# Retention attention into a squared-ReLU feed-forward: smaller loads and memsets, a later copy and sum, and two start-up casts on ScalarE

## The chip, the cores and the metric

The kernel runs on one core of a Trainium2 chip. The metric is the device time of one execution in microseconds (us). A core has five engines that run their own instruction streams in order and meet through semaphores: TensorE (PE, with its weight loads shown apart as PEld), VectorE (DVE), ScalarE (ACT), GpSimd (POOL) and SyncE (SP, which here only issues transfers). Transfers run on the core's 16 DMA engines.

## The reference, cut to what matters

Two stages. The first is a recurrent attention over 4 batches, 8 heads, 768 tokens and 64 channels; the second is a feed-forward layer over all 3072 tokens.

```python
gamma = 1.0 - 2.0 ** (-5.0 - np.arange(H))            # one decay for each head
for t in range(S):
    state = gamma * state + outer(k[t], v[t])         # 64 x 64 for each batch and head
    y[t] = scale * q[t] @ state
x = y.transpose(0, 2, 1, 3).reshape(B * S, H * D)     # 3072 x 512
h = np.maximum(x @ w_in, 0.0)                         # w_in: 512 x 2048
out = h * h @ w_out                                   # w_out: 2048 x 512
```

## The kernel before

The recurrence is computed in chunks of 128 tokens, 24 in all. Inside a chunk the attention is a masked product of scores and v; between chunks a state is carried in PSUM (`c_ps`) and copied to bf16 (`s_bd`). The decays are folded into q, k and, later, v, by scaling them with powers of gamma. The results `xt` of a block of chunks feed the feed-forward: `first_product` (L847) multiplies by w_in, ACT applies the ReLU (L856), DVE squares (L827), and the second product multiplies by w_out. The first block holds four chunks, the others two each.

The second product of a pair of chunks is made from seven half-size products and sums of their operands. For the first block this is `last_of_first`: it treats chunks 2 and 3 this way, and chunks 0 and 1 plainly (`plain`, L1043). Its sums are made on DVE by `add` (L1004) in `first_sums`, `third_sums` and `fourth_sums`; `fourth_sums` makes s4 in two halves, x = 0 and 1, which only the last product reads. Its results leave through ACT copies to `osb` tiles and stores on SP.

Start-up. All of q's, k's and v's first four chunks come in pairs. PE multiplies by the zero tile `still` between real products (`keep_awake`, L368), which computes nothing. `cast_pair_v` (L597) casts v to bf16, by default on POOL, one call for each of two row sets r; its argument `on_scalar` would use ACT. `state_pair` (L653) needs both. `cast_w` casts a 512 x 512 group of w_in in two column halves of four chunks each, one letter per chunk: G is POOL, V is DVE, S (any other) is ACT. The first half of the first group is cast as "GGGV".

The rest is a written order. Each piece of the feed-forward is a step of a generator (`ffn_pieces`), counted by n. `put(place, what, ...)` notes work, such as a load, a scaling, a transpose, that is issued behind piece number `place`; `before(n)` issues it, in the order of the `put` calls. So each engine's stream follows from the places. `attend(5, ...)` puts the transposes of k (`transpose_k`, L430, with two ACT copies to `k_bd` at L437) at place 27, the two halves of `scores` (L456 on PE, masked by DVE at L463) at places 30 and 32, and the outputs (L532) at 34. The scores' PSUM pool `ps_st` has one buffer, so the second half of the scores waits for the mask of the first.

Loads: `load_q(m)` (L93) loads q for two chunks, 512 KB, in one transfer on SP's queue; `load_kv` (L126) loads k or v of a chunk. `load_w_out` goes through POOL's queue. The pool memsets at L1372 clear the unused half of three `k_big` tiles, one instruction for each half of the partitions.

Of the kernel before, what the change touches and what calls it, by code (L numbers as in the profile page):

```python
# [13 lines left out]
AF = mybir.ActivationFunctionType  # L14
ALU = mybir.AluOpType
# [16 lines left out]
def kernel(  # L32
# [9 lines left out]
    nc = tc.nc  # L42
# [4 lines left out]
    C = 128  # L47
# [37 lines left out]

    raw_q, raw_k, raw_v = {}, {}, {}

    def load_q(m):

        b, i = chunks[m]  # L90
        t = ldqpool.tile([P, H, 2, D], FP32, name="qn")
        src = q[b, :, i * C : (i + 2) * C, :].rearrange("h (s r) d -> s h r d", r=2)
        nc.sync.dma_start(t[:], src)  # L93
        raw_q[m] = t

    heads_of = [slice(0, H // 2), slice(H // 2, H)]
# [250 lines left out]
    def cast_w(kind, g, halves=(0, 1), on="VVSG"):  # L347

        src = staged[kind, g]
        dst = (w_in_bf if kind == "in" else w_out_bf)[g]  # L350
        for half in halves:
            c = slice(half * 256, (half + 1) * 256)
            for j, engine in enumerate(on):
                if engine == "G":
                    nc.gpsimd.tensor_copy(dst[:, j, c], src[:, j, c])
                elif engine == "V":
                    nc.vector.tensor_copy(dst[:, j, c], src[:, j, c])
                else:
                    nc.scalar.activation(dst[:, j, c], src[:, j, c], AF.Copy)
# [3 lines left out]
    def keep_awake(n, width=4 * C, pool=ps_f, name="psf"):  # L363
        if not idle_ps:
            idle_ps.append(pool.tile([P, 4, P], FP32, name=name))
        wide = max(1, width // C)
        for _ in range(n):
            nc.tensor.matmul(  # L368
                idle_ps[0][:, 0:wide, 0 : width // wide],
                lhsT=still,  # L370
                rhs=still[:, None, 0 : width // wide].to_broadcast([P, wide, width // wide]),
                start=True,
                stop=True,
            )
# [217 lines left out]
    def cast_pair_v(m, r, on_scalar=False):  # L592
        at[m]["v"] = pair_view(v_bd2s[m // 2])
        if on_scalar:
            nc.scalar.activation(at[m]["v"][:, r], raw_v[m][:, r], AF.Copy)
        else:
            nc.gpsimd.tensor_copy(at[m]["v"][:, r], raw_v[m][:, r])  # L597
# [385 lines left out]
    def last_of_first():  # L983

        def halves_of(k, c):
            return [
                t.rearrange("e (j k) (c t) -> e k c j t", k=2, c=4)[:, k, 2 + c] for t in h2s[0]
            ]

        (a11, a12), (a21, a22) = ([halves_of(k, c) for k in range(2)] for c in range(2))  # L990
        n = NFB // 4
        s1, s2, s4 = (
            [
                t.rearrange("e (x j t) -> e x j t", x=2, t=C)[:, x]
                for x in range(2)
            ]
            for t in (spare[:, i * HN * 4 : (i + 1) * HN * 4] for i in range(3))
        )
        s3 = a21
        b = lambda k, c: lambda j: w_out_bf[j // 2][:, 2 * (j % 2) + k, c * HN : (c + 1) * HN]  # L1000
        t1, t2, t3, t4 = (lambda j, t=t: t[:, j] for t in sums)

        def add(out, in0, in1, op=ALU.add):
            nc.vector.tensor_tensor(out=out, in0=in0, in1=in1, op=op)  # L1004

        def product(to, left, right, js, start=True, stop=True):
            for j in js:
                nc.tensor.matmul(  # L1008
                    to,
                    lhsT=left[j // n][:, j % n],  # L1010
                    rhs=right(j),
                    start=(start and j == 0),
                    stop=(stop and j == NFB // 2 - 1),
                    skip_group_check=True,
                )

        def first_sums(x):
            add(s1[x], a21[x], a22[x])
            add(s2[x], s1[x], a11[x], ALU.subtract)

        def third_sums():
            for x in range(2):
                add(s3[x], a11[x], a21[x], ALU.subtract)

        def fourth_sums():
            for x in range(2):
                add(s4[x], a12[x], s2[x], ALU.subtract)

        def second_products():
            ops = [ps_f.tile([P, DM], FP32, name="psf") for _ in range(2)]  # L1030
            pa, pe, pd, pb = (
                t[:, n * HN : (n + 1) * HN]
                for t in [ps_f.tile([P, DM], FP32, name="psf") for _ in range(2)]
                for n in range(2)
            )
            oa, ob = (opool.tile([P, DM], FP32, name="osb") for _ in range(2))
            a, u, v = (upool.tile([P, HN], FP32, name=f"u{i}") for i in range(3))
            r0 = 2 * C

            def plain(j):  # L1040
                for f in (2 * j, 2 * j + 1):
                    for c, op in enumerate(ops):
                        nc.tensor.matmul(  # L1043
                            op[:],
                            lhsT=h_of(0, f)[:, 0, c * C : (c + 1) * C],
                            rhs=w_out_bf[f // FPQ][:, f % FPQ, :],
                            start=(f == 0),
                            stop=(f == NFB - 1),
                        )
                product(pa, a11, b(0, 0), (j,))  # L1050

            lo, hi = range(0, 4), range(4, 8)
            for j in range(4):
                plain(j)
                yield
            product(pd, s1, t1, lo)
            product(pb, s2, t2, lo, False)
            yield
            for j in range(4, 6):
                plain(j)  # L1060
                yield
            product(pe, a22, t4, lo, False)
            yield
            plain(6)
            yield
            plain(7)
            nc.scalar.activation(a[:], pa, AF.Copy)
            for c, op in enumerate(ops):
                osb = opool.tile([P, DM], FP32, name="osb")
                nc.scalar.activation(osb[:], op[:], AF.Copy)  # L1070
                nc.sync.dma_start(out[c * C : (c + 1) * C], osb[:])
            yield
            product(pd, s1, t1, hi)
            product(pb, s2, t2, hi)
            add(u[:], pb, a[:])
            yield
            product(pa, a12, b(1, 0), lo, False)
            yield
            product(pa, a12, b(1, 0), hi, False)
            nc.scalar.activation(oa[:, 0:HN], pa, AF.Copy)  # L1080
            yield
            product(pb, s3, t3, lo, False)
            yield
            product(pb, s3, t3, hi, False)
            add(v[:], pb, a[:])
            add(ob[:, HN:DM], pd, v[:])
            yield
            product(pe, a22, t4, hi)
            add(ob[:, 0:HN], pe, v[:])

            def last_product():
                product(pd, s4, b(1, 1), range(8), False)
                add(oa[:, HN:DM], pd, u[:])
                yield
                nc.sync.dma_start(out[r0 + C : r0 + 2 * C], ob[:])
                yield
                nc.sync.dma_start(out[r0 : r0 + C], oa[:])
                yield

            kept.append(last_product())  # L1100
            yield

        return first_sums, (third_sums, fourth_sums), second_products
# [27 lines left out]
    def ffn_pieces(tb):  # L1131
        nch = BLOCKS[tb]
        TB = nch * C
        if tb == 0:
# [1 line left out]
            put(11, first_sums, 0)  # L1136
            put(17, first_sums, 1)
            put(26, last_sums[0])
            put(27, last_sums[1])
            for f in range(FPQ, NFB):  # L1140
                hp = ps_f.tile([P, TB], FP32, name="psf")
                first_product(tb, hp[:], f, slice(0, TB))
# [97 lines left out]
    mask_b(0)  # L1240
    mask_b(1)
    keep_awake(1)
    transpose_pair_k(2, 1, *f)
    cast_pair_v(0, 0)
    cast_pair_v(0, 1)
    cast_pair_v(2, 0)
    cast_pair_v(2, 1)
    mask_a = scores_pair(2, 0, (st, f), spare[:, 0:1024])
    keep_awake(2)
    end_awake()  # L1250
    mask_a(0)
    mask_a(1)
# [2 lines left out]
    outputs_pair(0, 1)  # L1255
    mask_b = scores_pair(2, 1, (tp, f), spare[:, 1024:2048])
    mask_b(0)
    cast_w("in", 0, (0,), "GGGV")
    mask_b(1)
    finish_pair(0, 0)  # L1260
    finish_pair(0, 1)
    state_pair(0, 1, "SV")
    outputs_pair(2, 0, ((ps_y, "y"), st))
    first_pair(0)
# [20 lines left out]
    def put(place, what, *args):  # L1285
        parts.setdefault(place, []).append((what, args))
# [31 lines left out]
        put(place, load_w_out, g)  # L1318
    for m, which, place in ((4, "v", 10), (5, "k", 12), (5, "v", 14)):
        put(place, load_kv, m, which)  # L1320
    put(15, load_q, 6)
    for m, which, place in ((6, "k", 16), (6, "v", 17), (7, "k", 18), (7, "v", 19)):
        put(place, load_kv, m, which)
    put(10, cast_w, "in", 3)
# [15 lines left out]

    for j, t in enumerate(k_bigs):
        for hh in range(2):
            put((16, 34, 43)[j] + hh, nc.gpsimd.memset, t[halves[hh], :, :, 1 - hh, :], 0.0)

    put(20, load_q, 8)
    put(41, load_q, 10)
    done = [57, 62] + [70 + 8 * j for j in range(14)]

    ahead = {
# [62 lines left out]
```

## Time and profile before

| what | value |
|---|---|
| median of 3 runs | 203.47 us (203.37 to 203.81) |
| profiled execution, its own time | 203.39 us |
| its span (first to last instruction) | 201.6 us |
| busy: PE, PEld | 195.0, 164.6 us |
| busy: DVE, ACT, POOL | 151.0, 127.1, 82.7 us |
| moved by DMA | 36.02 MB, mean 179 GB/s |
| L368 warming matmuls before L653 | two, at 11.44 us on the chain |
| L430 transposes of chunk 5 | 43.06 us on the chain |

Times inside the profile count from the start of the span. Busy time of PE includes the modelled end of each pipelined matmul, so PE shown busy is not PE at its peak. A group of instructions is named by line, engine, operation, tile written and tiles read. The chain that ended last follows the end of the program back, at each step to what released it.

### The profile page before, as it was taken

The page shows a single profiled execution, that of the slowest core. Times are in us where ns is not written, and L with a number is a line of the kernel's source. Part 1 is how long each engine was busy: PE and PEld are TensorE (multiplying, and loading weights), DVE is VectorE, ACT ScalarE, POOL GpSimd, SP SyncE. Part 2 cuts the span into 40 slices and gives each one's busy share as a digit, 9 for nine tenths or more (in the row PEclk, how much of TensorE's full clock was granted, in tenths as well). Part 3 has the DMA queues.
Part 4 walks back from the last instruction along what each step waited for, and adds up shares of the span by engine and source line. Part 5 has one row for each costly group of instructions (what it writes and reads, how often), then busy time and mean ns, then how long its engine had stood idle before and what let it go on. Part 6 is the DMA issues. An engine that isn't in the chain of part 4 may idle for free.

```text
span 201.6 us, 5846 instructions
## 1 busy us (share of the span) xinstructions
PE 195.0 (97%) x2362; PEld 164.6 (82%) x2362; DVE 151.0 (75%) x327; ACT 127.1 (63%) x258; POOL 82.7 (41%) x150
## 2 busy tenths in 40 slices
PE   7799999999999999999999999999999999999991
PEld 2468445779988999899999999999999999999881
DVE  3986899799598886777687697697696696484472
ACT  8864875264863666774766866864865865845710
POOL 8683760899930762154422185116362202200000
PEclk9999999999999999999999999999999999999999
DMA  5999999999987999599979399999999762101102
GB/s 166 356 375 397 343 192 196 252 201 227 305 174 182 176 163 238 172 134 180 189 152 206 114 170 221 158 242 141 192 153 140 197 94 67 66 0 52 55 0 106
DMA packets 92250, 36.02 MB, mean 179 GB/s; under 512 B 68544, under 2 KB 88256, under 8 KB 92224
## 3 DMA queue, kind: packets, MB, share of 16 engines
q1 hardware_dynamic: 73088, 31.47, 66.5%
q0 software_dynamic: 19136, 4.20, 23.3%
q8 instruction: 18, 0.29, 0.6%
q14 instruction: 8, 0.07, 0.1%
HBM read 27.26 MB, written 6.29 MB: 166 GB/s over the span
## 4 chain that ended last, share of the span: by engine, by line
PE 91%; DVE 4%; DMA 2%; issue 1%; ACT 0%; DVEq 0%
PE psf L847 42%; PE psf L884 21%; PE tp L884 7%; PE psf L1043 3%; PE psf L1008 2%; DMA qn<-in_q_dram 2%; PE y L804 2%; PE st L748 2%; PE y L797 2%; PE c_ps L775 2%; PE c_ps L653 1%; PE y L532 1%; PE st L456 1%; PE y L368 1%; DVE qs L559 1%; DVE osb L880 1%
## 5 line engine op out<-in xcount | busy, mean ns | idle before, releaser
L847 PE MATMUL psf<-xt,w_in_bf 128*128 128x256 bf16 (+2 forms) x864 | 92.3, 261 | 0.0
L847 PEld LDWEIGHTS <-w_in_bf 128*128 128x128 bf16 x864 | 70.8, 98 | 11.2
L856 ACT ACTIVATE h<-psf 128x512 bf16<-128x512 f32 x96 | 56.2, 594 | 24.3 <-PE psf L847 22.0
L726 POOL COPY v_bd<-v 64x512 bf16<-64x512 bf16 x32 | 21.7, 677 | 76.5 <-DVE v L718 75.6
L827 DVE TENSOR_TENSOR h<-h 128x512 bf16<-128x512 bf16 x80 | 32.8, 423 | 19.1 <-ACT h L856 18.4
L884 PEld LDWEIGHTS <-h 128*128 128x128 bf16 x344 | 31.7, 98 | 3.7 <-issue 0.2
L156 POOL DMA_DIRECT2D k_big<-in_k_dram x40 | 26.6, 686 | 0.1
L884 PE MATMUL psf<-w_sum,h 128*128 128x256 bf16 x168 | 23.5, 273 | 0.0
L884 PE MATMUL tp<-w_out_bf,h 128*128 128x256 bf16 x136 | 19.1, 273 | 0.0
L880 DVE TENSOR_TENSOR u<-psf,u 128x256 f32<-128x256 f32 x20 | 8.5, 424 | 12.7 <-PE psf L884 11.8
L884 PE MATMUL psf<-w_sum,k_bd 128*128 128x256 bf16 x144 | 17.9, 273 | 0.0
L880 DVE TENSOR_TENSOR osb<-psf,u 128x256 f32<-128x256 f32 x29 | 11.4, 420 | 6.6 <-PE psf L884 6.3
L884 PEld LDWEIGHTS <-k_bd 128*128 128x128 bf16 x144 | 13.8, 98 | 1.5
L784 ACT ACTIVATE s_bd<-c_ps 64x256 bf16<-64x256 f32 x29 | 10.7, 369 | 6.3 <-PE c_ps L775 6.3
L387 DVE TENSOR_TENSOR qs<-qn,qf 128x512 bf16<-128x512 f32 x20 | 13.7, 688 | 0.0
L785 ACT ACTIVATE s_bd<-c_ps 64x256 bf16<-64x256 f32 x29 | 11.0, 379 | 0.4
L755 DVE TENSOR_TENSOR pt<-st,cmask 128x512 bf16<-128x512 f32 x16 | 11.0, 687 | 0.2
L718 DVE TENSOR_TENSOR v<-stage,kf 128x512 bf16<-128x512 f32 x16 | 10.9, 683 | 0.0
L920 ACT ACTIVATE osb<-tp 128x256 f32<-128x256 f32 x8 | 3.1, 384 | 12.2 <-PE tp L884 12.2
L811 ACT ACTIVATE xt<-y 128x512 bf16<-128x512 f32 x16 | 9.6, 598 | 1.8 <-PE y L804 1.2
L825 ACT ACTIVATE h<-h 128x512 bf16<-128x512 bf16 x16 | 10.1, 630 | 0.5
L880 DVE TENSOR_TENSOR k_bd<-h 128x512 bf16<-128x512 bf16 x18 | 9.9, 553 | 0.3
(147 smaller groups left out, 290.1 us busy)
## 6 DMA issues: line engine op xcount, KB each, us to landing
qn<-in_q_dram SPq DMA_DIRECT2D x12, 512.0 KB, 5.7
out_dram<-osb SPq DMA_DIRECT2D x23, 256.0 KB, 2.6
stage<-in_v_dram SPq DMA_DIRECT2D x32, 96.0 KB, 3.9
stage<-in_moe_w_in_dram SPq DMA_DIRECT2D x4, 512.0 KB, 6.8
stage<-in_moe_w_in_dram SPq DMA_DIRECT2D x2, 1024.0 KB, 10.7
w_out_bf<-in_moe_w_out_dram POOLq DMA_DIRECT2D x4, 512.0 KB, 10.4
kn<-in_k_dram SPq DMA_DIRECT2D x6, 256.0 KB, 6.2
k_big<-in_k_dram POOLq DMA_DIRECT2D x32, 48.0 KB, 3.8
```

Source lines behind the costliest of these rows:

```text
L156: nc.gpsimd.dma_start(t[rows, 2 * at_w : 2 * (at_w + size), p, hh, :], half_rows(k, b, 2 * p + hh, i + w, size),)
L387: engine.tensor_tensor(out=out, in0=by, in1=table[:, :, None].to_broadcast([P, H, D]), op=ALU.mult)
L718: nc.vector.tensor_tensor(out=v2.rearrange("s (u p) d -> s u p d", u=2), in0=vn, in1=kf2[:, i, :, :, None].to_broadcast([P, 2, NPAIR, D]), ...
L726: nc.gpsimd.tensor_copy(v_bd[rows, :, hh, :], v2[rows])
L755: nc.vector.tensor_tensor(out=pt[:], in0=st[:], in1=cmask2.rearrange("s r t -> s (r t)")[:, None, :].to_broadcast([P, 2 * NPAIR, C // 2]), ...
L784: nc.scalar.activation(s_bd[halves[0], :, 0, :], c[halves[0]], AF.Copy)
L785: nc.scalar.activation(s_bd[halves[1], :, 1, :], c[halves[1]], AF.Copy)
L827: nc.vector.tensor_mul(hv, hv, hv)
L847: nc.tensor.matmul(hp, lhsT=w_in_bf[g][:, cb, fq * 128 : (fq + 1) * 128], rhs=xts[tb][:, cb, cols], start=(cb == 0), stop=(cb == NCB - 1),)
L856: nc.scalar.activation(hv, hp[:], AF.Relu)
L880: nc.vector.tensor_tensor(out=out, in0=in0, in1=in1, op=op)
L884: nc.tensor.matmul(to, lhsT=left[:, j], rhs=right(j) if callable(right) else right[:, j], start=(start and j == 0), stop=(stop and j == NF ...
```

## The change

Six edits, all before 62 us of the profile:

- the loads of q for chunks 6, 8 and 10 are each made in two transfers, by heads;
- the memsets of the `k_big` tiles are each made in two pieces, at the same places;
- the second of two output copies of the first block, with its store, is issued two steps later, behind the work of place 27;
- the second half of `fourth_sums` moves from place 27 to place 30;
- the first v is cast half on POOL and half on ACT, ahead of a transposition's copy on ACT, and one of two warming matmuls behind it is left out;
- the third chunk of the first half of w_in's first group is cast on ACT, behind the copies of the first two chunks' outputs, instead of on POOL.

```diff
-    def load_q(m):
+    def load_q(m, heads=(slice(0, H),)):
...
-        src = q[b, :, i * C : (i + 2) * C, :].rearrange("h (s r) d -> s h r d", r=2)
-        nc.sync.dma_start(t[:], src)
+        for part in heads:
+            src = q[b, part, i * C : (i + 2) * C, :].rearrange("h (s r) d -> s h r d", r=2)
+            nc.sync.dma_start(t[:, part], src)
...
             for j, engine in enumerate(on):
+                if engine == "-":
+                    continue
...
-        def fourth_sums():
-            for x in range(2):
-                add(s4[x], a12[x], s2[x], ALU.subtract)
+        def fourth_sums(x):
+            add(s4[x], a12[x], s2[x], ALU.subtract)
...
             nc.scalar.activation(a[:], pa, AF.Copy)
-            for c, op in enumerate(ops):
+
+            def store(c):
                 osb = opool.tile([P, DM], FP32, name="osb")
-                nc.scalar.activation(osb[:], op[:], AF.Copy)
+                nc.scalar.activation(osb[:], ops[c][:], AF.Copy)
                 nc.sync.dma_start(out[c * C : (c + 1) * C], osb[:])
+
+            store(0)
             yield
             product(pd, s1, t1, hi)
             product(pb, s2, t2, hi)
             add(u[:], pb, a[:])
             yield
+            store(1)
...
-            put(27, last_sums[1])
+            put(27, last_sums[1], 0)
+            put(30, last_sums[1], 1)
...
     keep_awake(1)
+    cast_pair_v(0, 0)
+    cast_pair_v(0, 1, on_scalar=True)
     transpose_pair_k(2, 1, *f)
-    cast_pair_v(0, 0)
-    cast_pair_v(0, 1)
     cast_pair_v(2, 0)
     cast_pair_v(2, 1)
     mask_a = scores_pair(2, 0, (st, f), spare[:, 0:1024])
-    keep_awake(2)
+    keep_awake(1)
...
-    cast_w("in", 0, (0,), "GGGV")
+    cast_w("in", 0, (0,), "GG-V")
     mask_b(1)
     finish_pair(0, 0)
     finish_pair(0, 1)
+    cast_w("in", 0, (0,), "--S-")
...
-    put(15, load_q, 6)
+    put(15, load_q, 6, heads_of)
...
-            put((16, 34, 43)[j] + hh, nc.gpsimd.memset, t[halves[hh], :, :, 1 - hh, :], 0.0)
+            for to in (t[halves[hh], 0:4], t[halves[hh], 4:]):
+                put((16, 34, 43)[j] + hh, nc.gpsimd.memset, to[:, :, :, 1 - hh, :], 0.0)
...
-    put(20, load_q, 8)
-    put(41, load_q, 10)
+    put(20, load_q, 8, heads_of)
+    put(41, load_q, 10, heads_of)
```

## The prediction

> **What bounds the kernel now.** I read the page first: which engine is full, where the chain that ended last runs, and the granted clock.
>
> ```profile
> span 201.6 us, 5846 instructions
> PE 195.0 (97%) x2362; PEld 164.6 (82%) x2362; DVE 151.0 (75%) x327; ACT 127.1 (63%) x258; POOL 82.7 (41%) x150
> ...
> PEclk9999999999999999999999999999999999999999
> ...
> PE 91%; DVE 4%; DMA 2%; issue 1%; ACT 0%; DVEq 0%
> ```
>
> TensorE (PE) is busy 195.0 of 201.6 us at full clock, and the chain is PE's own stream for 91%. So an edit counts only if it shortens PE's stream or closes one of its few gaps. The list of PE's waits names no stop after 46.1 us, and between 64.1 and 190 us the table by stretches gives PE 125.90 busy of 125.90. Every edit here lies before 62 us, so what PE gains or loses early is carried to the end unless a later wait takes it back. I then read the chain in order of time at the two places the edits touch. The columns are start, duration, what. The start-up:
>
> ```profile
> 11.44 0.54 PE y L368 x2
> 11.97 0.56 PE c_ps L653 x8
> ...
> 12.56 0.38 ACT s_bd L664
> ...
> 13.38 0.40 PE psf L693 x4
> ```
>
> The first state product (L653) starts when PE has finished two warming matmuls (L368) that compute nothing; behind it the chain is strict: two ScalarE (ACT) copies, at 12.56 and 12.95, then PE. The second place:
>
> ```profile
> 43.06 0.24 PE tp L430 x4
> 43.30 0.04 issue
> 43.34 0.42 DVE u L1004
> 43.77 0.60 DVE w_sum L345
> 44.36 1.08 DVE h L1004 x2
> 45.45 0.61 DVE pt L463
> 46.06 0.04 issue
> 46.10 0.38 PE st L456 x4
> ```
>
> Here the chain leaves PE for 2.8 us and runs through VectorE (DVE): an add, a weight sum, the two fourth sums (h), and the mask of the scores (pt), which frees the only st buffer for the next scores (L456). That is the largest stop of PE behind the start. It has a second cause, from the timelines of the weight loads (PEld), ACT and POOL (idle time and what ended it in brackets):
>
> ```profile
> 44.72 0.17 PEld L456 LDWEIGHTS <-k_bd 128*128 128x128 bf16 x3 [0.30 <-ACT k_bd L437]
> 42.51 1.08 ACT L1070 ACTIVATE osb<-psf 128x512 f32<-128x512 f32 x2
> 43.46 1.21 ACT L437 ACTIVATE k_bd<-tp 64x512 bf16<-64x512 bf16 x2
> 10.58 1.16 POOL L597 CAST v_bd<-vn 128x512 bf16<-128x512 f32 x2
> ```
>
> The k_bd copies stand behind two output copies; in the start-up the first v is cast on POOL in two pieces, ending at 10.58 + 1.16 = 11.74.
>
> **Start-up.** One warming matmul of the pair goes. A pair takes 0.43 at 7.06 on the chain, so one is 0.215. Gone, PE could start L653 at 11.97 - 0.215 = 11.75 on the chain, with its row at 11.91 - 0.215 = 11.69. With both v casts still on POOL (11.74) that would gain about 0.15 of it; so the cover has to move too. After: POOL casts the first half, 10.58 to 11.19. ACT casts the second after its kT copy of 10.22 (597 ns), from about 10.76. The v load was issued at 3.53 and took 7.0 to land, 10.53, so ACT does not wait. No row shows ACT casting 128x512 from f32 in SBUF; the nearest are 630 ns (L825, SBUF to SBUF, bf16) and 594 (L856, f32 from PSUM). I take 0.63, end 11.39; even at 0.9 it ends at 11.66, in time. The kT copy behind it moves from 11.13 to about 11.35 and ends at 11.95; its reader on PE starts near 12.65: hidden with 0.7 to spare, and beyond that it would stop PE. Gain 0.21.
>
> The third w_in chunk goes from POOL to ACT. On POOL it ended at 13.46 + 1.15 = 14.61. On ACT it stands behind xt (13.85, now 13.64), can start at 14.16, and takes 406 ns (L359, same shape): 14.57. PE's first product starts at 14.61 - 0.21 = 14.40 and loads the third chunk's weights two matmuls of 0.123 later, 14.64. It just fits; if not, it costs up to 0.15 (an ACT step of 0.55). Behind it on ACT the half state copy (14.37) slips to 14.5; its reader starts at 15.7. POOL's 0.38 saved is worth nothing, since each later w_in cast there waits for its transfer (idle of 0.20, 1.98, 0.52, 1.76).
>
> **The copy later.** ACT's second output copy, one step of 0.5, no longer precedes the k_bd copies. They can start when PE ends the transposes, 42.90 + 0.39 = 43.29, at 43.33 instead of 43.46: 0.13 earlier, end 44.54. The copy itself then runs 44.4 to 45.0 and the next (L1080) to 45.3; ACT's next work waits for PE until 47.4. The PSUM buffer it frees is next written at 47.66. Its store, on SP, waits until 45.0; the next on SP is a store of 48.39. All hidden.
>
> **The sum later.** One of the two fourth sums (0.42; the other shows 0.83) moves behind the mask and two q scalings. The mask then waits for the scores alone. Those end at 44.43 + 0.63 = 45.06, now 44.93; mask 44.98 to 45.66 instead of 45.37 to 46.05; PE's L456 at 45.71 instead of 46.10. Gain 0.39, the 0.13 of the copy included. PE's own stream would allow 45.67, so no more. What is late next: on DVE the sum lands before the adds of 47.17 and the mask of 48.29. Old spacings (0.60 a scaling, 0.34 to 0.45 a sum) put the adds at 47.1 to 48.3 and the mask at 48.24 to 48.92; PE wants its result at 49.48 - 0.39 = 49.09. It fits by 0.15.
>
> **Loads of q in halves.** Three more issues on SP. 256 KB issues of the same run length take 0.49 (L115, row of 1.25), a whole q 0.57 to 0.59 when nothing holds it: +0.4 each, from both sides: not below zero, and not above one more held issue of 4.5. q(6) is issued at 31.65, lands 10.5 later at 42.15 and is first read at 45.97. Behind it in SP's queue k(6) lands at 43.05 and is read at 48.88; q(10), 57.84 + 4.3, is read after 66: all hidden. The built program also holds a load on SP until the one eight before it on that queue has landed, so a split moves that distance by one; the eighth before k(6), a w_in load, had been cast by 25.0. The Trainium skill, DMA: Bandwidth & Descriptors, section Measured (HBM→SBUF, 128 partitions, SWDGE, issued from GpSimd), speaks against the split: batch transfers to 1 MiB or more. By it these loads land later; the sum stays, as long as the slack of over 3 us holds. **Memsets in halves**: 64x512 takes 0.52 and 64x2048 1.80, so 0.83 ns an element and 0.09 fixed: 6 x 0.09 = 0.54 on POOL, which sits idle 8.78 before 66.19. Zero.
>
> **Sum.** 0.21 + 0.39 = 0.60, less 0.05 for the third chunk's tight fit: 0.55. The profiled execution took 203.39 (201.6 and 1.8 around it): 202.84. The median 203.47 is 0.08 above it: forecast 202.9. About 0.2%, 0.41 us, is what a measurement of this kernel can tell from no change.
>
> **Rivals.** *The moved sum is held up* (0.15). One fourth sum took 0.83 where its twin took 0.42, a weight sum at 35.27 took 1.10 where others take 0.68, and ks at 40.94 took 1.10 against 0.68: each 0.41 late, with POOL casting v or issuing k loads. The moved sum starts near 46.6, beside POOL's v cast (46.83, 0.89). Held by 0.41 it pushes the mask's end to 49.33 against 49.09: 0.29 lost of the 0.39, so 0.31 in all, 203.15. Against it: it would start before the cast. The Trainium skill, SBUF — State Buffer, section Who interferes with whom, says a VectorE instruction with two SBUF inputs and a GpSimd one that reads SBUF lock each other out, the first to start winning; by that rule the sum goes first.
>
> *The gain is given back* (0.13). PE arrives earlier and waits for w_out: group 2 lands at 24.99 + 11.1 = 36.09 and is first used at 36.58, group 3 at 39.45 against 40.08, and their issue does not move. Slack 0.49 and 0.63, less 0.21. If w_out takes the start-up's gain and the first product waits as well, 0.1 to 0.4 remains: 203.2. That the change does not do what it says, PE still held at 11.97 by the casts, leaves the 0.39: 203.1; it lies in here.
>
> *Slower* (0.17): the halves of q(6) let SP's transfers crowd w_out. From 30 to 45 us the DMA engines are full, and w_out took 7.0 to 11.5 to land, so 1.5 us more is within the spread. It decides once group 3 lands later than 40.08 + 0.39 + 0.41 = 40.9, 1.45 later than now; at 41.5 the loss is 1.4 less 0.39: 204.5. At 41.0 it is 0.5. Against it: halves carry the same bytes on the same queue. The warming matmul belongs here only by the clock, and the granted clock is 9 in all slices, with PE busy around it.
>
> **Numbers.** Forecast 0.55, own range 202.7 to 203.05 (the 0.15 and 0.13 terms either way); held sum 0.15; given back 0.13; slower 0.17. Faster by over 0.2% is the forecast and a part of the third case: 0.60. Slower 0.17. Within 0.2%: 0.23. The range reaches from the forecast's best, 202.6 with the doubtful 0.05 and a run's scatter, to 203.6, short of most of the slow case.
>
> **What would show it.** In the chain, one L368 before L653 and L653 near 11.7; L847's first product near 14.4 with no gap at its third weights; L456 at 45.5 in the new clock of the span with no DVE sum ahead of the mask; outputs(5) near 48.9; then every row about 0.55 earlier and the span near 201.05. Wrong if PE shows a wait between 31 and 42, if DVE's moved sum takes 0.8, or if rows after 64 us are not earlier.

## The result, and the profile after

The changed kernel takes 202.87 us, median of 22 runs (202.83 to 203.88), beside 203.44 for the kernel before (22 runs, 203.21 to 203.81). The ratio is 0.9972, interval 0.9965 to 0.9978: faster by 0.28%, 0.57 us. Its profiled execution took 202.86, 0.53 less than that of before (203.39). 202.9 was forecast. The total is right; two of its parts are not, as the rows below show, and their errors nearly cancel.

In the changed kernel's line numbers most helpers stand 3 lines further down: L368 is L371, L430 L433, L456 L459, L653 L656, L1004 L1007. The page of the changed kernel:

```profile
span 201.1 us, 5856 instructions
...
PE 194.7 (97%) x2361; PEld 164.6 (82%) x2361; DVE 151.0 (75%) x327; ACT 128.0 (64%) x260; POOL 81.9 (41%) x154
...
PE 91%; DVE 3%; DMA 2%; ACT 1%; issue 1%; DVEq 0%
```

TensorE is as full as before. In the chain DVE has lost a point and ACT has one: the stop in the middle of the kernel now runs through ScalarE. The chain in order of time, start-up and second place (start, duration, what):

```profile
11.43 0.32 PE y L371
11.75 0.56 PE c_ps L656 x8
...
12.33 0.38 ACT s_bd L667
...
13.16 0.40 PE psf L696 x4
...
42.83 0.24 PE tp L433 x4
...
43.71 0.59 ACT k_bd L440
44.30 0.02 issue
44.32 0.19 ACT osb L1073
44.52 0.30 issue
44.82 0.39 ACT osb L1086
45.20 0.04 issue
45.25 0.60 PE psf L1011 x4
45.84 0.22 PE st L459 x4
```

In the start-up one warming matmul (L371) is left, and the state product starts at 11.75 where it started at 11.97: 0.22 gained, and the transposes (row of L433: 42.67, before 42.90) still have it. A row is a group's own start in the timeline; the chain counts a piece only from where the one before it ends, so the two differ by up to 0.2. At the second place no sum and no mask is on the chain any more. The chain goes from the k_bd copies through the moved output copy (L1073) and ACT's next copy (L1086, into `oa`) to four products of L1011, which write the other half of the PSUM tile that this copy reads. That wait was not in the prediction. The second scores of L459 start at 45.68 by their row (46.10 before): 0.42 in all, of which 0.23 is the start-up's and 0.19 this place's. From there everything is 0.41 earlier: outputs at 49.07 instead of 49.48, the start of the last two stores on SP at 197.23 instead of 197.64. The missing 0.12 of the 0.53 lies behind those stores; that is the last experiment.

The timelines of ACT, DVE and POOL at these places (in brackets idle time and what ended it):

```profile
10.84 0.63 ACT L598 ACTIVATE v_bd<-vn 128x512 bf16<-128x512 f32 x1
14.10 0.42 ACT L362 ACTIVATE w_in_bf<-stage 128x256 bf16<-128x256 f32 x1
...
44.73 0.69 DVE L466 TENSOR_TENSOR pt<-st,cmask 128x512 bf16<-128x512 f32 x1 [0.27 <-PE st L459]
46.54 0.42 DVE L1007 TENSOR_TENSOR h<-h,h 128x512 bf16<-128x512 bf16 x1
46.60 0.83 POOL L406 CAST v_bd<-vn 128x512 bf16<-128x512 f32 x1
```

The cast of v on ACT took the 0.63 that was assumed, and the third w_in chunk was done at 14.52. The mask (L466) waits for the scores alone. The moved sum (h, 46.54) took 0.42 and ran just ahead of POOL's cast.

### The profile page after: what moved, and what is told of

The parts are those of the page before. It is cut to its first block, busy times and chain, and to the rows that moved or that the text cites. A ratio compares the mean times of both kernels' runs of the same rounds, so it can differ in the third digit from the quotient of the medians.

```text
span 201.1 us, 5856 instructions
## 1 busy us (share of the span) xinstructions
PE 194.7 (97%) x2361; PEld 164.6 (82%) x2361; DVE 151.0 (75%) x327; ACT 128.0 (64%) x260; POOL 81.9 (41%) x154
## 4 chain that ended last, share of the span: by engine, by line
PE 91%; DVE 3%; DMA 2%; ACT 1%; issue 1%; DVEq 0%
PE psf L850 42%; PE psf L887 21%; PE tp L887 7%; PE psf L1045 3%; PE psf L1011 2%; DMA qn<-in_q_dram 2%; PE st L751 2%; PE y L807 2%; PE y L800 2%; PE c_ps L778 2%; PE c_ps L656 1%; PE y L535 1%; PE st L459 1%; DVE qs L562 1%; PE y L371 1%
```

## Experiments

Twelve kernels ran, each in several rounds beside the kernel before. "Outputs" is the first y of outputs(5), in before at 49.48; "second scores" the second group of L456 or L459, in before at 46.10. In the expectations the first theory is: 0.22 from the warming matmul; 0.20 from sum and copy, with PE then waiting for ACT's copy of oa; nothing from loads and memsets.

**The start-up part alone.** The kernel before with this:

```diff
+    cast_pair_v(0, 0)
+    cast_pair_v(0, 1, on_scalar=True)
     transpose_pair_k(2, 1, *f)
-    cast_pair_v(0, 0)
-    cast_pair_v(0, 1)
...
-    keep_awake(2)
+    keep_awake(1)
...
-    cast_w("in", 0, (0,), "GGGV")
+    cast_w("in", 0, (0,), "GG-V")
...
+    cast_w("in", 0, (0,), "--S-")
```

> The start-up edits alone (ACT casts half of the first v and one w_in chunk, one warming matmul less); loads, memsets, copy and sum as before. First theory: PE's first state product starts 0.22 earlier and every later row with it, L456 of 46.10 near 45.88, time lower by 0.2 to 0.25. Rival, the smaller loads and memsets carry part of the gain: the same here, but then the parts alone leave 0.1 or more for them. Rival, w_out holds PE when it comes earlier: a wait between 31 and 42 us and a gain under 0.1.

Measured: 203.15 (ratio 0.9988, 0.9973 to 1.0002, so the times alone do not settle it; the rows do). State product at 11.71 by its row (11.91 before), transposes 42.70, second scores 45.92, outputs 49.30. The 0.20 is there and passes through w_out's stretch to the end without a stop.

**One warming matmul less, and nothing else.**

```diff
-    keep_awake(2)
+    keep_awake(1)
```

> The kernel before with one warming matmul less and nothing else, so both halves of the first v are cast on POOL, ending at 11.74. First theory: the state product starts at 11.82 to 11.87 on the chain, a gain of 0.1 to 0.15, so the cast on ACT is worth the remaining 0.07 to 0.12. Rival, PE alone sets the start: the full 0.22.

Measured: 203.25 (0.9988, 0.998 to 0.9997). The state product starts at 11.73 on the chain, although both casts of v are still on POOL; the transposes come at 42.77, 0.13 early. The profiled execution (203.05) is among the fastest of this kernel, 0.20 under the median, so its later rows flatter it. Most of the start-up's gain needs only the matmul gone. Of what is lost by the transposes, 0.04 is in the state product (0.60 on the chain for 0.56). Another 0.08 is in PE's first product (1.06 for 0.98), whose weight loads stop for the third w_in chunk, here still cast on POOL:

```profile
14.70 0.55 PEld L847 LDWEIGHTS <-w_in_bf 128*128 128x128 bf16 x6 [0.18 <-POOL w_in_bf L355]
```

**Both warming matmuls, all else as changed.**

```diff
-    keep_awake(1)
+    keep_awake(2)
```

> The changed kernel with both warming matmuls back. First theory: the state product is at 11.97 on the chain again and the time 0.22 above the changed kernel, 203.08; the casts on ACT alone give nothing. Rival, the casts give the gain: 202.9.

Measured: 203.09 (0.9979, 0.9971 to 0.9988); the chain has L371 x2 and L656 at 11.96, second scores at 45.90, the last stores' row 0.22 later than in the changed kernel. The matmul is worth 0.22, from the start-up to the end.

**The sum alone.** In the kernel before:

```diff
-            put(27, last_sums[1])
+            put(27, last_sums[1], 0)
+            put(30, last_sums[1], 1)
```

> Only the second fourth sum moves, from place 27 to 30; the copy stays. First theory (the copy's move makes a new wait of PE for ACT): the mask starts when the scores end, 45.06, and L456 at 45.83 instead of 46.10, a gain of 0.27, more than sum and copy together give. Rival, the recorded prediction's step (the copy's move is worth 0.13 on top): 0.26 here, and 0.39 with the copy. Rival, the moved sum is held by POOL: 0.1 or less at the outputs near 49.4.

Measured: 203.48 (1.0015, 0.9996 to 1.0033), no gain. The second scores come at 45.82, 0.28 early as expected, but outputs at 49.54, 0.06 late. The timelines of DVE and POOL say where it went:

```profile
46.88 0.89 DVE L1004 TENSOR_TENSOR h<-h,h 128x512 bf16<-128x512 bf16 x1
...
48.81 0.68 DVE L463 TENSOR_TENSOR pt<-st,cmask 128x512 bf16<-128x512 f32 x1
...
46.78 0.70 POOL L403 CAST v_bd<-vn 128x512 bf16<-128x512 f32 x1
```

The moved sum starts 0.10 behind POOL's cast and takes 0.89 instead of 0.42; adds and mask slip behind it. This is the prediction's first rival: it happens here, and not in the changed kernel, where the sum starts 0.06 ahead of the cast and the cast takes the loss (0.83). The Trainium skill, SBUF — State Buffer, section Who interferes with whom, has the first to start win; both traces agree with that by their rows. The price is not the same on either side: the sum loses 0.47 (0.89 for 0.42), the cast 0.13 (0.83 for the 0.70 that it takes here).

**The copy alone.** In the kernel before, the second output copy moved behind the products:

```diff
-            for c, op in enumerate(ops):
+
+            def store(c):
                 osb = opool.tile([P, DM], FP32, name="osb")
...
+            store(0)
             yield
...
             add(u[:], pb, a[:])
             yield
+            store(1)
```

> The kernel before with the second output copy moved behind the products, and nothing else. First theory: the mask still waits for the two fourth sums on DVE, which the copy does not touch, so the second L456 stays at 46.0 to 46.1; the moved copy is done by 45.0, before PE can come to the products that need ACT's copy of oa; time 203.35 to 203.45, no change. Rival (the copy is what freed PE): L456 at 45.9, time 203.2. Second rival (the moved copy costs by itself, since it stands ahead of the oa copy on ACT): outputs 0.1 to 0.2 later than 49.48, 203.5 to 203.6.

Measured: 203.68 (203.29 to 204.54; ratio 1.0, 0.9981 to 1.0019). No gain: the chain still goes through the two fourth sums and the mask. In its profiled execution the second scores are at 45.98, but outputs at 49.73, 0.25 late, with DVE's two q scalings taking 1.77 beside POOL's cast where they take 1.28 in the changed kernel. Whether that is usual for this kernel, the wide scatter leaves open.

**Sum and copy.** Both of the last two edits in the kernel before.

> Sum and copy moved, start-up, loads and memsets as before. First theory: PE waits about 0.3 for ACT's copy of oa, which now stands behind the moved output copy; L456 of 46.10 near 45.90, gain 0.20, less than the sum alone. The prediction's step: 45.71, gain 0.39.

Measured: 203.26 (0.999, 0.9978 to 1.0002); second scores 45.89, outputs 49.27, 0.21 early; the chain goes through ACT's osb and oa copies as in the changed kernel. At the scores that is 0.07 later than with the sum alone, so there the moved copy costs 0.07 instead of bringing the 0.13 forecast. What it brings is indirect: the moved sum starts at 46.81 and keeps its 0.41, while the cast takes 0.90.

**The copy one step further.** The changed kernel, with the moved copy behind ACT's copy of oa:

```diff
-            store(1)
             product(pa, a12, b(1, 0), lo, False)
...
             nc.scalar.activation(oa[:, 0:HN], pa, AF.Copy)
+            store(1)
```

> The changed kernel with its moved copy and store one step later still, behind ACT's copy of oa. First theory (PE waits for the copy of oa, held by the moved copy): the wait at 45.25 of the changed kernel is gone, L459 there at 45.47 instead of 45.68, time lower than the changed kernel by 0.2 (202.67). Rival, PE waits at that place for its own stream or for DVE: L459 stays at 45.6 to 45.7 and the time at 202.87.

Measured: 202.65 (0.9959, 0.9947 to 0.9972). The chain in order of time:

```profile
43.07 1.31 PE psf L1011 x12
44.38 0.33 PE st L459 x4
44.72 0.87 PE psf L1011 x8
45.59 0.29 PE st L459 x4
```

No ACT piece is left: PE runs from the transposes through both score groups. Second scores by their row at 45.50, outputs 48.88, last stores 0.19 earlier than in the changed kernel. So the 0.2 missing at the second place is PE waiting for the copy of oa behind the moved copy. The 45.5 and the 48.9 that the prediction named for the changed kernel are met by this one.

**And no warming matmul there at all.**

```diff
-    keep_awake(1)
     end_awake()
```

> As copy_last, and the last warming matmul ahead of the first state product is left out too. If warming matmuls in the way are what the start-up gain is made of, PE starts the state product when the ACT cast of v ends, 10.84 + 0.63 = 11.47, so near 11.53 instead of 11.75: 0.2 lower than copy_last. Rival, ACT's kT copy behind the cast, then the state copies, are the bound: under 0.1. Rival, the clock falls without it: PE clock under 1.0 in the first slices and time above by 1 or more.

Measured: 202.45 (five runs, 202.41 to 202.50; ratio 0.9946, 0.9932 to 0.996), the fastest kernel of this study, 0.42 under the changed one. The chain:

```profile
11.43 0.65 PE c_ps L656 x8
12.08 0.02 issue
12.10 0.38 ACT s_bd L667
```

The state product now starts as soon as PE is free, 8 of them in 0.65 instead of 0.56, and ACT's copies start 0.23 earlier than in the changed kernel. The granted clock's mean was 0.995 and the runs agree, so nothing shows that PE needed that matmul to keep its clock.

**Loads and memsets alone.**

> Only the loads of q in halves and the memsets in halves. First theory: no row of PE moves, time the same within 0.1, although k(6) is issued some 3 us later on SP. Rival, they carry the part of the gain that the rows of PE do not show: 0.1 to 0.2 lower. Rival, they delay w_out: a wait of PE between 36 and 41 us and a time above by 0.2 or more.

Measured: 203.26 (202.92 to 205.25; 1.0011, 0.9989 to 1.0033): unclear. The profiled execution took 202.92, the fastest of twelve, with both fourth sums at their short 0.42 and outputs at 49.13. Its rows are therefore not typical. They do show that the stop at the second place is not there in every execution: a weight sum at 41.44 took 1.10 here where it takes 0.68 in before, both fourth sums were short behind it, and the second scores came at 45.75 with nothing changed at that place. The profiled execution of one_warm_pool shows the same (1.09, and 45.71).

**All but loads and memsets.** The changed kernel with these lines as before:

```diff
-    put(15, load_q, 6, heads_of)
+    put(15, load_q, 6)
...
-            for to in (t[halves[hh], 0:4], t[halves[hh], 4:]):
-                put((16, 34, 43)[j] + hh, nc.gpsimd.memset, to[:, :, :, 1 - hh, :], 0.0)
+            put((16, 34, 43)[j] + hh, nc.gpsimd.memset, t[halves[hh], :, :, 1 - hh, :], 0.0)
...
-    put(20, load_q, 8, heads_of)
-    put(41, load_q, 10, heads_of)
+    put(20, load_q, 8)
+    put(41, load_q, 10)
```

> The changed kernel with q loaded whole and the memsets whole, as before; start-up, copy and sum as changed. First theory: the splits bring nothing and cost nothing that PE sees, so PE's rows stand where the changed kernel has them, the second mask-freed scores (L456 of before, 45.68 after) at 45.6 to 45.75, outputs at 49.0 to 49.1, time 202.85 to 202.95. Rival: the splits carry the 0.10 to 0.15 us by which the medians differ more than PE's rows; then 203.0 to 203.05 with the same rows. Second rival: the splits shift POOL and DVE against each other where they hold each other up (40 to 47 us); then one of the sums at 44.0 or 46.5 takes 0.82 where it took 0.42 or the other way round, and outputs move by 0.2 to 0.4.

Measured: 202.97 (202.93 to 203.03; 0.997, 0.9958 to 0.9981), 0.10 over the changed kernel's median. Second scores 45.74 and outputs 49.13, 0.06 later, which the state product's row has already (11.74 against 11.68). Behind the start of the last two stores this kernel needs 5.74 (203.03 less 197.29), the changed one 5.63 (202.86 less 197.23). So the splits move nothing that PE sees, and about 0.11 at the end of the program.

**The same for the fastest kernel.** copy_last_no_warm with whole loads and memsets.

> The changed kernel with the moved copy behind ACT's copy of oa, with no warming matmul ahead of the first state product, and with q and the memsets whole as before. First theory: as with the splits, 202.45, scores of L456 at 45.3, outputs at 48.7. Rival (splits carry 0.10 to 0.15): 202.55 to 202.6. Second rival (POOL and DVE held differently): rows 0.2 to 0.4 off from the second site on.

Measured: 202.60 (0.9957, 0.9942 to 0.9972), 0.15 over the one with the splits. The profiled execution took 203.19, well above the median, with the transposes at 43.01, so its rows are not compared; behind the last stores it needs 5.77, its counterpart 5.64.

**Three other loads split.** What comes behind the last stores stands like this in the profiled executions (own time less the start of the last two stores on SP):

| kernels | loads of q | POOL instructions | us behind the last stores | of these, to POOL's closing instruction | from it to the end of the span |
|---|---|---|---|---|---|
| before, sum_alone, copy_alone, copy_sum_alone, one_warm_pool | whole | 150 | 5.75 to 5.79 | 3.5 | 0.4 |
| startup_alone, whole_loads, best_whole | whole | 148 | 5.74 to 5.77 | 3.1 | 0.9 |
| changed, copy_last, copy_last_no_warm, two_warm | split | 154 | 5.61 to 5.64 | 3.4 | 0.4 |
| loads_memsets_alone | split | 156 | 5.63 | 3.4 | 0.4 |
| late_halves | split, later ones | 148 | 6.09 | 3.4 | 0.9 |

POOL's closing instruction is the one `EVENT_SEMAPHORE_RANGE_CLEAR` of each program; the two last columns are from the traces' own times, rounded, and the remaining 1.8 lies outside the span in all fourteen. The last line is the experiment, whose edit against best_whole is this, with load_q as in the changed kernel:

```diff
-            put(d - 29, load_q, m)
+            put(d - 29, load_q, m, heads_of if m < 18 else (slice(0, H),))
```

> best_whole with three other loads of q in halves (q(12), q(14), q(16), issued between 64 and 110 us) instead of q(6), q(8), q(10); memsets whole. In the profiled runs so far the time behind the issue of the last two stores (own time less their start on SP) is 5.61 to 5.64 in the five kernels with the split loads and 5.74 to 5.79 in the eight with whole ones, whatever else differs. First theory: three DMAs more on SP's queue move the last store to another of the eight lanes that SP's transfers take in turn (the built program makes it wait on lane 2 here and with the change, on lane 7 with whole loads), and the end of the program comes 0.13 earlier behind it: 5.61 to 5.64 here too, median 202.45 to 202.5. Rival: it comes from the split loads of 31 to 62 us or from the memsets, by what they leave behind: 5.74 to 5.79, median 202.55 to 202.65.

Measured: 202.90 (202.87 to 203.59; 0.9978, 0.9969 to 0.9988). Neither theory: its rows are those of copy_last_no_warm to 0.04 (outputs 48.66 against 48.69), and behind the last stores it needs 6.09, 0.45 more. The timeline of SP of late_halves, whose own time is 202.91:

```profile
196.82 0.83 SPq L981 DMA_DIRECT2D out_dram<-osb  x2
```

and that of copy_last_no_warm, whose own time is 202.50:

```profile
196.86 0.83 SPq L981 DMA_DIRECT2D out_dram<-osb  x2
```

The stores are issued 0.04 earlier and the execution is 0.41 longer. Both make as many transfers, and the last store waits on the same lane (semaphore 104 in both traces), so the lane does not decide. The two programs differ in which loads are split and in the memsets (6 instructions on POOL). The record shows where the 0.45 lies. POOL's closing instruction in late_halves, whose span is 201.1:

```profile
L1414 POOLq EVENT_SEMAPHORE_RANGE_CLEAR  x1: 139/139/139, 200.2 to 200.2; - x1
```

and in copy_last_no_warm, whose span is 200.7:

```profile
L1415 POOLq EVENT_SEMAPHORE_RANGE_CLEAR  x1: 139/139/139, 200.3 to 200.3; - x1
```

So 0.9 follows it against 0.4. The last two columns of the table show two parts that neither theory had told apart: the part behind POOL's closing instruction is 0.9 in the four programs with 148 instructions on POOL and 0.4 in the ten others, and the part ahead of it is 3.4 in all six programs with split loads, early or late, and 3.1 or 3.5 with whole ones. late_halves has the 3.4 of the one kind and the 0.9 of the other. Why a program's make-up should set these parts stays open. One more difference shows: between 196 and 203 us the queue that the page calls `q14 instruction` moves one packet in the five programs at 5.61 to 5.64 and two in the nine others, but two stand at 5.75 as well as at 6.09, so the count alone does not set the length.

## Why the prediction was right, and where it was not

**Start-up, 0.21: right.** 0.22 on the chain, 0.23 at the transposes, 0.22 between two_warm and the changed kernel. The cover held: 0.63 for the cast. The third w_in chunk was done at 14.52 for 14.57 forecast, and PE's first product shows no gap, so the 0.05 allowed for it was not needed. The reason given for moving the v cast did not hold as stated: with both casts on POOL (one_warm_pool) the state product still started at 11.73, not at the 11.82 that a gain of 0.15 means, and its matmuls took only 0.04 longer. That 0.13 reached the transposes there, near the 0.15 named, is luck: the other 0.08 was lost to the third w_in chunk on POOL, so its move, which the sum had as a cost of 0.05, is a gain of about that size.

**Second place, 0.39: 0.19 measured.** The sum's own part was right: 0.39 less the copy's 0.13 is 0.26, and sum_alone gave 0.28 at the scores. The step that failed is "All hidden" of the moved copy. It asked what waits for that copy (its buffer, its store) and when ACT's next work waits for PE, and did place the next copy (L1080 there) "to 45.3"; it did not ask who on PE waits for that next copy. Four products do, and the second scores stand behind them in PE's order. The 0.13 became a cost of 0.07; copy_last takes it away and lands on 45.50.

**Loads and memsets, zero: right for PE, wrong for the time.** q(6) in two pieces held SP for 7.26 instead of 4.50, within the bound given. k(6) behind it was issued at 39.12 instead of 36.25, but its issue then took 0.45 instead of 3.45, and no one waited for it. But the program's end is 0.12 shorter with these splits (5.63 against 5.75), a term that the sum did not have: the "1.8 around it" held, while the time from the last stores to the end of the span, which was taken as constant, did not. The sum over the profiled executions is now closed: 0.23 + 0.19 less 0.01 by the end, and 0.12 behind the last stores, make the 0.53. That the forecast own time (202.84) came within 0.02 is the accident of 0.20 too much here, 0.12 too little there and 0.05 of unneeded allowance.

**Rivals.** *The moved sum held up* is real but not in this kernel: sum_alone shows it, at a higher price than forecast (0.34 between scores and outputs, for 0.29), and a start 0.06 ahead of POOL's cast is, by the rows, what the changed kernel is safe by. *The gain given back at w_out* did not happen: what the start-up gained arrives at the transposes in full. *Slower by crowded transfers* did not either, by the same rows. The Trainium skill, DMA: Bandwidth & Descriptors, section Measured (HBM→SBUF, 128 partitions, SWDGE, issued from GpSimd), speaks for large batches, and the prediction took from it that the split loads land later. The trace does not agree for these loads on SP's queue: whole, q(6) landed at 42.15; its halves, issued at 31.77 and 36.68, took 9.4 and 5.3 and landed at 41.2 and 42.0, and k(6) behind them landed at 42.9 instead of 43.05. No run here shows the rate of one transfer alone.

## What to carry to other kernels

When a step moves to another place on an engine that works in order, list what then stands behind it, and for each of those who waits on the engine that sets the time, not only who waits for the moved step. Where two engines' work holds each other up with a margin of a tenth of a microsecond, price both orders: an edit that gains 0.28 at one place may return it all at the next, and a second edit that costs by itself may save it. At a quarter of a per cent, compare the time behind the last store as well as the rows before it.

## What the runs showed of the hardware

Two things were not expected. When a VectorE sum of two SBUF tiles meets a POOL cast, one of them takes longer, and which one turns on about 0.1 us in their starts: 46.54 against 46.60 and the cast took 0.83 for 0.70, 46.88 against 46.78 and the sum took 0.89 for 0.42. In copy_sum_alone the sum kept its 0.41 from 46.81 with the cast's row at 46.79 and 0.90 long, so starts this close are not told apart by the rows. And the program's end behind the last stores is a property of the built program: 5.61 to 5.64, 5.74 to 5.79 or 6.09 us in fourteen programs, whatever happened before it. It has a part of 0.4 or 0.9 behind POOL's closing instruction and one of 3.1 to 3.5 ahead of it, in differing combinations; what sets them is not shown.
